# Block 2's second product in a fused retention and feed-forward kernel: from eight block products to seven

## The chip, the cores and the metric

The kernel runs on one core of a Trainium2 chip. The metric is the device time of one execution in microseconds (us). Before the change it is 290.14 us, the median of 3 runs (290.06 to 290.16). The engines are called by the profile's names: PE (TensorE, matrix products), PEld (its weight loads), DVE (VectorE), ACT (ScalarE), POOL (GpSimd) and SP (SyncE, which here only issues DMA transfers, in its program's order).

## The reference

For 8 batches, 8 heads, 576 positions and head width 64, the attention part is retention: scores without softmax, damped by a power of the distance. Its result, as 4608 rows of 512, goes through a feed-forward layer of width 2048 with the activation h / (1 + exp(-beta h)).

```python
scores = (1 / sqrt(64)) * q @ k.T                    # per batch and head
ret = scores * where(i >= j, gamma[head] ** (i - j), 0)
x = (ret @ v)                                        # heads side by side: 4608 x 512
h = x @ w_in                                         # 4608 x 2048
g = h / (1 + exp(-beta * h))
out = g @ w_out                                      # 4608 x 512
```

Inputs and output are float32; the kernel multiplies in bfloat16.

## The kernel before

**Blocks.** The rows are worked on in nine blocks of 512. Blocks 0 to 7 are the first 512 positions of each batch, block 8 is the last 64 positions of all eight. For each block m, `up` (L773) makes the first product: 16 pieces (`fo`) of 128 columns of width 2048, each 4 matmuls of 512 columns into a PSUM bank of tag `mm`, of which there are three; ACT reads the bank, applies the activation (L790) and writes the piece of `gT` in bfloat16. In block 1 the first ten pieces are done in two halves of 256 columns (L1026).

**The second product in two ways.** For blocks before `SB` (L50, here 3: blocks 0 to 2), `down` (L901) makes `out = g @ w_out` with 64 matmuls of 512 columns (L908), ACT or DVE copies each finished bank to `ot` (L915), and SP stores it. From block `SB` on, the product is cut into 2 x 2 quarters and made from seven products of sums of quarters instead of eight (Strassen's method, in a form that needs few sums): `seven_mm` (L809), 7 x 16 matmuls of 256 columns (L820), on sums of the quarters of `gT` (`seven_a`, L798, DVE) and sums of the quarters of `w_out` (`seven_b`, L239), and `seven_out` (L825) combines the results on ACT and DVE. In these blocks the odd pieces of `gT` get an extra scaling on DVE by a ratio of betas, by way of a scratch buffer `hs` (L785 to L788).

**The weight sums** are made once, for four groups g of `w_out` rows. For each group, `scale_w_out` scales four float32 tiles in place on ACT (L237), `seven_b` makes five sums on DVE (L254) and two negated copies on ACT (L250), and `last_seven` (L256) gives the float32 tile back. The sums of group 0 have a place of their own; those of groups 1 to 3 take the buffers that the float32 tiles of groups 0 to 2 leave (tag `wt`), and `hs` takes that of group 3. The sums of `gT` take the place of `w_out_sb`, the plain bfloat16 weights (tag `wo`), which `cast_w_out` (L222) has made in block 0.

**Attention.** The attention of batch b is computed while block b-1 is in work, in between the large matmuls. `load_q` (L77) and `load_kv` (L89) bring its inputs; POOL scales and casts them (`pre_q` L322, `pre` L342); `x_q` and `x_k` (L403, L406) have the DMA engines transpose them; `scores` (L615) makes the scores of one or both pairs of chunks and the states of four chunks; DVE masks the scores (L298 stands for all steps that are recorded through the helper `F` there) and sums the states (`fold`, L590), whose bfloat16 copies ACT or DVE makes; `both4` (L708) makes outputs and cross terms, and writes the block's `xT`. `first_states` (L607) makes the first four states of a batch by themselves; `crosses4` otherwise makes those of the next batch along with the cross terms (L687). In the first two batches other functions do the same with transposes on PE (`t_q`, `t_k`, L413, L420; `a_sc`, L434; `state_out`, L534; `second`, L1038).

**The order.** Each engine works through its instructions in the program's order. That order is written by hand: `fill` is a list of positions, each a few large matmuls, and `streams` are lists of (position, step); `merged` (L928) puts each step ahead of the first `fill` entry whose index is not below its position. `d0` is the first position of block 0's second product, `u1 = d0 + 16` the start of block 1, `base[n]` the start of block n, and `base[2] = u1 + 42`, called T in the prediction. A `down` block has 16 + 16 positions, a seven-product block 16 + 14. Batch n+1's preparation is placed by `pair_prep` (L1067) relative to `at` (L1137 to L1141), its scores at `base[n] + lead[n]` from block `SB` on (L1109), and the transpose of its second pair by `asked` (L1112). `release` (L897) stores four held-back pieces of the output of blocks 0 and 1.

Of the kernel before, what the change touches and what calls it, by code (L numbers as in the profile page):

```python
# [19 lines left out]
def kernel(  # L20
# [11 lines left out]
    B, H, S, D = q.shape  # L32
# [14 lines left out]


    blocks = list(range(B + 1))
    SB = 3  # L50
    KH = FO // 2
    NH = d_model // 2
    seven = (3, 4, 1, 5, 2, 7, 6)
# [19 lines left out]
    XB = 2  # L73
# [65 lines left out]
    for j, (steps, mul) in enumerate((([[2, 2], [1, 2]], CB), ([[2 * P, 2], [1, 2]], 2))):  # L139
        nc.gpsimd.iota(pos[:, j, :CB].rearrange("p (a r) -> p a r", r=2), pattern=steps, base=0, channel_multiplier=mul,  # L140
                       allow_small_or_imprecise_dtypes=True)
        for x in range(2):
            nc.gpsimd.iota(pos[x * TL:(x + 1) * TL, j, CB:CB + 1], pattern=[[0, 1]], base=MB, channel_multiplier=1,
                           allow_small_or_imprecise_dtypes=True)
            for m, base in ((0, TL), (1, x * P)):
                nc.gpsimd.iota(pos[x * TL:(x + 1) * TL, j, CB + 1 + 2 * m:CB + 3 + 2 * m], pattern=[[2 * P, 2]],
                               base=x * TL + base, channel_multiplier=1, allow_small_or_imprecise_dtypes=True)
# [40 lines left out]
    WG = 4  # L188
# [108 lines left out]
    def F(f, *a):  # L297
        return lambda: f(*a)  # L298
# [291 lines left out]
    def fold(b, e, bank, ns=range(4), casts=None, by=None):  # L590

        for n in ns:
# [5 lines left out]
            else:  # L598
                nc.vector.tensor_tensor(ends[b][:], of, new, ALU.add)
                return  # L600
            cast = F(by or (nc.vector.tensor_copy if b > SB else nc.scalar.copy), sbq[e + n], to)
            if casts is not None:
# [165 lines left out]


    gts = {}  # L770
    halved = (12, 13, 14, 15)

    def up(m, fo, c0=0, cn=CB):  # L773
        if m not in gts:
            gts[m] = sb.tile([P, FO, CB, P], BF16, name="gT", tag="gT", bufs=1)
        w = slice(c0 * PC, (c0 + cn) * PC)
        ph = psum.tile([P, CB, P], F32, name="ph", tag="mm", bufs=3)
        ph = ph.rearrange("f i s -> f (i s)")[:, :cn * P].rearrange("f (i s) -> f i s", i=CB)
        ns = 2 if m == SB and fo in halved or m == 1 and 10 <= fo < 13 else 1
        for ko in range(KO):  # L780
            for n in range(ns):
                cs = slice(n * CB // ns, (n + 1) * CB // ns)
                nc.tensor.matmul(ph[:, cs], w_in_sb[:, ko, fo * P:(fo + 1) * P], xts[m][:, ko, cs, w],  # L783
                                 start=(ko == 0 and n == 0), stop=(ko == KO - 1), skip_group_check=ns > 1)
        if m >= SB and fo % 2:  # L785
            h = scratch[0][:, fo // 2 % 4].rearrange("f (i s) -> f i s", i=CB)
            nc.scalar.activation(h, ph, ACT.Silu, scale=beta_sb[:, fo:fo + 1])  # L787
            nc.vector.tensor_scalar(gts[m][:, fo], h, ratio[:, fo // 2:fo // 2 + 1], None, ALU.mult)  # L788
            return
        nc.scalar.activation(gts[m][:, fo, :, w], ph, ACT.Silu, scale=beta_sb[:, fo:fo + 1])  # L790
# [224 lines left out]
    d0 = len(fill)  # L1015
# [9 lines left out]
    u1 = len(fill)  # L1025
# [3 lines left out]
    base = {1: u1 + 10}  # L1029
# [37 lines left out]
    def pair_prep(i, at):  # L1067
        b, c = seq[i]
        if b is None:
            if c:  # L1070
                return [(at - 27, F(load_tail, c)), (at - 20, F(load_tail, c + 1)), (at - 17.5, F(pre, i)),
                        (at - 12, F(pre, i + 1)), (at - 12, F(x_tail, i)), (at - 9.5, F(x_tail, i + 1))]
            return [(at - 31, F(load_tail, c)), (at - 21.5, F(pre, i)), (at - 21, F(load_tail, c + 1)),
                    (at - 13, F(pre, i + 1)), (at - 12, F(x_tail, i)), (at - 9.5, F(x_tail, i + 1))]
        n, st = full.index(i), []
        if b == XB:
            if c == 0:
                return [(d0 + 13, F(pre, i + x, (0,))) for x in range(2)] + \
                       [(d0 + 14, F(pre, i + x, (1,))) for x in range(2)]
            return [(u1 + 8 + x / 2, F(pre, i + x)) for x in range(2)]  # L1080
        if c == 0:
            st += [(at - 30, F(x_k, XB, 1))] if b == XB + 1 else []
            st += [(at - 30, F(load_q, b))] + [(at - 20 + x, F(pre_q, b, x)) for x in range(4)]
            st += [(at - 14 + 1.5 * x, F(x_q, b, x)) for x in range(2)]
            return st + [(at - 28, F(load_kv, n)), (at - 26, F(load_kv, n + 1)), (at - 16, F(pre, i)),
                         (at - 15, F(pre, i + 1)), (at - 11.5, F(x_k, b, c // 2))]
        turned_at = asked[b + 1] - 30.1
        st += [(turned_at - 0.4 + 0.1 * x, F(pre, i + x, (0,))) for x in range(2)]
        st += [(turned_at, F(x_k, b, c // 2))] + [(turned_at + 0.1 + 0.1 * x, F(pre, i + x, (1,))) for x in range(2)]
        return st + [(at - 29.3, F(load_kv, n)), (at - 29.2, F(load_kv, n + 1))]  # L1090

    def span(a, n, by=1.0):
        return [a + by * x for x in range(n)]

    sums_b = (3, 4, 1, 7, 6)
    t = base[2]
    by_scalar = [span(t - 15.5, 4, 0.8), span(t - 12, 4, 0.8), [t - 9.7, t - 9.4, t - 9.1, t - 3.6], span(t + 16.5, 4, 0.7)]
    by_vector = [span(t - 11, 5, 1.4), span(t - 3, 5, 1.5), span(t + 4.5, 5, 1.8), span(t + 19.6, 5, 1.4)]
    negated = [(t - 3.8, t - 3.4), (t + 0.5, t + 2.5), (t + 16.1, t + 16.2), (t + 21, t + 23)]
    for g in range(WG):  # L1100
        streams.append([(x, F(scale_w_out, g, i)) for i, x in enumerate(by_scalar[g])])
    streams.append(sorted([(x, F(seven_b, g, j)) for g in range(WG) for xs, js in ((by_vector[g], sums_b), (negated[g], (2, 5)))
                           for x, j in zip(xs, js)] +
                          [(max(by_vector[g][-1], negated[g][-1]) + 0.1, F(last_seven, g)) for g in range(WG)], key=lambda x: x[0]))

    def queued(at, steps):
        return [(x, lambda: steps.pop(0)()) for x in at]

    lead = dict(zip(range(SB, B - 1), (7, 4, 2, 1)))  # L1109
    lead[B - 1] = 5  # L1110
    behind = dict(zip(range(SB, B - 1), (0, 0, 1, 0)))
    asked = {n + 1: base[n] + (lead[n] - 13 if n in lead else 3) for n in range(XB, B - 1)}  # L1112
    asked[B] = base[B - 2] + lead[B - 2] + 19

# [2 lines left out]
    for n in range(SB, B + 1):  # L1117
        t, m = base[n], blocks[n]
        first, second = slice(0, KH // 2), slice(KH // 2, KH)
        if n == SB:  # L1120
            halves = [(t + 14.4, 1, first), (t + 15.1, 5, first), (t + 16.3, 1, second), (t + 16.4, 5, second)] + \
                     [(t + 17.5 + 0.5 * x, j, ks) for x, (j, ks) in enumerate((j, ks) for j in (2, 7) for ks in (first, second))]
        else:
            early = [t + 11.4, t + 12.6, t + 15.3, t + 15.4] if n == SB + 1 else [t + 9.8, t + 10.8, t + 11.8, t + 14.4] if n < B else span(t + 9, 4)
            halves = [(x, j, first) for x, j in zip(early, (1, 5, 2, 7))] + [(t + 16.4 + 0.1 * x, j, second) for x, j in enumerate((1, 5, 2, 7))]
        streams.append([(x, F(seven_a, m, j, ks)) for x, j, ks in halves] +
                       [(t + 22.1, F(seven_a, m, 6))])

    todo = list(range(2 * CB, len(seq), 2))
    for n in range(1, B):  # L1130

        take = [i for i in todo if seq[i][0] == n + 1 or n == B - 1]
        todo = todo[len(take):]
        b, t = n + 1, base[n]
        t0 = t + lead.get(n, 0)
        if n == 1:
            at = [t + 17, base[b] - 8.3]  # L1137
        elif n < SB:
            at = [t + 3, t + 18]
        else:  # L1140
            at = [t0 - 13, t0 + 2] if n < B - 1 else [t0 - 9.5, t0 - 2.5]  # L1141
        for i, x in zip(take, at, strict=True):
            streams.append(pair_prep(i, x))
        if n == 1:
            streams.append([(d0 + 6.1, F(mask, late, [1, CB], [CB, PC // 2])),
                            (d0 + 6.2, F(mask, tri, [1, TL]))])
            streams.append([(at[0], F(group1, b, (0,))), (at[1], F(group1, b, (1,))), (at[1] + 4.1, F(both4, b))])
        elif n < SB:
            streams.append([(t + 16, F(first_states, b))] * (b == XB + 1) +
                           [(t + 19, F(group1, b, (0, 1))), (t + 25.9, F(both4, b))])  # L1150
        elif n == B - 1:
            outs = []
            streams.append([(t0, F(tail_scores, take[0])), (t + 13, F(both_tails, take[0], outs))] +
                           queued([t + 16.3, t + 17.6, t + 20.5, t + 22.5], outs))
        else:
            rest, outs = [], []
            t0 -= behind[n]
            if b == SB + 2 and SB == XB + 1:
                streams.append([(t - 4, F(first_states, b))])
            streams.append([(t0, F(scores, b, (0, 1), rest))] + queued([t0, t0 + 0.9, t0 + 1.7, t0 + 2.6, t0 + 3.4, t0 + 4.2, t0 + 4.3, t0 + 5.1, t0 + 6] if n == SB else  # L1160
                           [t0, t0 + 0.9, t0 + 0.9, t0 + 1.8, t0 + 2.6] + span(t0 + 3.4, 4, 0.9), rest))
            by = t + 17.4 if n == SB else t + 14.5 if n == SB + 1 else t + 12.8
            streams.append([(by, F(both4, b, outs))] + queued([t + 16.3 + 2 * (n == SB)] * 4 + [t + 17.3, t + 18.3, t + 20.3, t + 20.4][:0 if n in (SB, B - 2) else 4], outs))
    assert not todo
    merged(fill, *streams)

# [29 lines left out]
```

## Time and profile before

| | us |
|---|---|
| median of 3 runs | 290.14 (290.06 to 290.16) |
| the profiled execution, whole | 289.33 |
| its span in the profile | 287.6 |
| block 0's second product starts | 32.0 |
| block 1 starts | 49.8 |
| block 1's second product starts | 66.7 |
| block 2 starts | 83.5 |
| block 3 starts | 114.5 |
| block 4 starts | 143.8 |

The page of the profile gives the busy time of each engine, the groups of instructions and the chain of waits, which is followed back from the last instruction to what released each step. A group is "line, engine, operation, output <- inputs, shape, count | busy us, mean ns". The mean of a matmul is its latency (379 ns at 512 columns); matmuls follow each other more closely than that, so their spacing is read from the chain. In a timeline a line is "start, length, engine, line, operation, count, and in brackets the idle time before it with what ended it". `SPq` is the queue on which SP issues transfers; there the length is the time of the issue, not of the transfer. Windows are in us from the start of the span. The granted clock of PE is 1.00 all through.

### The profile page before, as it was taken

The page shows a single profiled execution, that of the slowest core. Times are in us where ns is not written, and L with a number is a line of the kernel's source. Part 1 is how long each engine was busy: PE and PEld are TensorE (multiplying, and loading weights), DVE is VectorE, ACT ScalarE, POOL GpSimd, SP SyncE. Part 2 cuts the span into 40 slices and gives each one's busy share as a digit, 9 for nine tenths or more (in the row PEclk, how much of TensorE's full clock was granted, in tenths as well). Part 3 has the DMA queues.
Part 4 walks back from the last instruction along what each step waited for, and adds up shares of the span by engine and source line. Part 5 has one row for each costly group of instructions (what it writes and reads, how often), then busy time and mean ns, then how long its engine had stood idle before and what let it go on. Part 6 is the DMA issues. An engine that isn't in the chain of part 4 may idle for free.

```text
span 287.6 us, 8701 instructions
## 1 busy us (share of the span) xinstructions
PE 278.9 (97%) x3618; PEld 177.2 (62%) x3648; DVE 185.3 (64%) x345; ACT 169.7 (59%) x298; POOL 132.3 (46%) x259
## 2 busy tenths in 40 slices
PE   7899999999999999999999999999999999999995
PEld 3564456884454455568854885578557845884584
DVE  5973546704797296289759856885698455742673
ACT  4567635686968882775358615681566166827730
POOL 7466019933991684195595476533089200000000
PEclk9999999999999999999999999999999999999999
DMA  7999999977899999999998998950779330012004
GB/s 224 306 364 386 382 310 294 178 160 208 168 184 264 244 186 210 291 212 191 194 260 212 181 269 249 197 116 0 230 168 156 87 136 3 2 46 100 2 7 139
DMA packets 120567, 54.05 MB, mean 188 GB/s; under 512 B 93888, under 2 KB 113360, under 8 KB 120528
## 3 DMA queue, kind: packets, MB, share of 16 engines
q1 hardware_dynamic: 120496, 53.49, 78.0%
q8 instruction: 28, 0.46, 0.7%
q14 instruction: 11, 0.09, 0.1%
q10 hardware_dynamic: 32, 0.01, 0.0%
HBM read 36.71 MB, written 9.44 MB: 160 GB/s over the span
## 4 chain that ended last, share of the span: by engine, by line
PE 94%; DMA 3%; issue 1%; SPq 1%; ACT 0%; POOL 0%; DVE 0%; ACTq 0%
PE ph L783 39%; PE po L908 14%; PE U L820 11%; PE Z L820 7%; PE W L820 7%; PE O L561 4%; PE ph L875 4%; DMA kvn<-in_k_dram 3%; PE sc L561 2%; PE st L561 2%; PE st L521 1%; PE ph L890 1%; PE T L425 1%; PE O L488 1%; SPq L86 0%
## 5 line engine op out<-in xcount | busy, mean ns | idle before, releaser
L783 PE MATMUL ph<-xT,w_in_sb 128*128 128x512 bf16 (+1 forms) x570 | 114.2, 354 | 0.9
L783 PEld LDWEIGHTS <-w_in_sb 128*128 128x128 bf16 x588 | 56.4, 98 | 52.1 <-DVE xT L694 0.2
L790 ACT ACTIVATE gT<-ph,beta_sb 128x512 bf16<-128x512 f32 (+1 forms) x92 | 58.2, 640 | 39.2 <-PE ph L783 38.1
L820 PEld LDWEIGHTS <-sa 128*128 128x128 bf16 x480 | 46.9, 98 | 5.5
L788 DVE TENSOR_SCALAR gT<-hs,ratio 128x512 bf16<-128x512 f32 x48 | 27.1, 565 | 31.2 <-ACT hs L787 30.7
L335 POOL TENSOR_TENSOR qs<-qn,gq 128x256 bf16<-128x256 f32 x48 | 29.9, 655 | 33.5 <-DMA qn<-in_q_dram 29.2
L787 ACT ACTIVATE hs<-ph,beta_sb 128x512 f32<-128x512 f32 x48 | 33.0, 687 | 18.9 <-PE ph L783 18.3
L908 PE MATMUL po<-w_out_sb,gT 128*128 128x512 bf16 x183 | 42.0, 379 | 1.0 <-issue 0.8
L804 DVE TENSOR_TENSOR sa<-gT 128x1024 bf16<-128x1024 bf16 (+1 forms) x54 | 41.6, 812 | 0.8 <-PE Z L820 0.6
L317 POOL TENSOR_TENSOR vn<-kvn,gv 128x256 bf16<-128x256 f32 x48 | 33.2, 715 | 3.0 <-issue 2.0
L372 POOL CAST kn<-kvn 128x128 bf16<-128x128 f32 (+1 forms) x72 | 25.1, 386 | 14.8 <-DMA kvn<-in_k_dram 14.7
L908 PEld LDWEIGHTS <-gT 128*128 128x128 bf16 x192 | 18.0, 97 | 20.8
L820 PE MATMUL Z<-b,sa 128*128 128x256 bf16 x192 | 22.9, 273 | 0.0
L820 PE MATMUL U<-b,sa 128*128 128x256 bf16 x192 | 22.9, 273 | 0.0
L298 DVE TENSOR_TENSOR R<-sc,late 128x512 bf16<-128x512 f32 x24 | 15.4, 679 | 11.3 <-issue 10.1
L820 PEld LDWEIGHTS <-gT 128*128 128x128 bf16 x192 | 18.7, 98 | 3.2
L254 DVE TENSOR_TENSOR b<-wt 128x512 bf16<-128x512 f32 x20 | 15.6, 840 | 1.9 <-ACT wt L237 1.8
L694 ACT CAST xT<-O 128x512 bf16<-128x512 f32 x19 | 9.8, 599 | 5.9 <-PE O L561 5.9
L384 POOL CAST kn<-kvn 128x512 bf16<-128x512 f32 x7 | 4.4, 647 | 16.0 <-DMA kvn<-in_k_dram 16.0
L820 PE MATMUL W<-b,gT 128*128 128x256 bf16 x96 | 11.5, 273 | 0.0
L820 PE MATMUL W<-b,sa 128*128 128x256 bf16 x96 | 11.5, 273 | 0.0
L820 PE MATMUL U<-b,gT 128*128 128x256 bf16 x96 | 11.5, 273 | 0.0
(122 smaller groups left out, 313.4 us busy)
## 6 DMA issues: line engine op xcount, KB each, us to landing
qn<-in_q_dram SPq DMA_DIRECT2D x16, 512.0 KB, 5.8
out_dram<-ot SPq DMA_DIRECT2D x32, 256.0 KB, 3.1
wt<-in_moe_w_out_dram SPq DMA_DIRECT2D x8, 512.0 KB, 9.2
kvn<-in_k_dram SPq DMA_DIRECT2D x12, 256.0 KB, 5.4
kvn<-in_v_dram SPq DMA_DIRECT2D x12, 256.0 KB, 6.2
kvn<-in_k_dram SPq DMA_DIRECT2D x24, 128.0 KB, 5.0
kvn<-in_v_dram SPq DMA_DIRECT2D x24, 128.0 KB, 4.1
wt<-in_moe_w_in_dram SPq DMA_DIRECT2D x5, 512.0 KB, 8.8
```

Source lines behind the costliest of these rows:

```text
L254: nc.vector.tensor_tensor(to, x, y, op)
L317: nc.gpsimd.tensor_tensor(vn[:, hs], v[:, hs], g[:, hs], ALU.mult)
L335: nc.gpsimd.tensor_tensor(batch[b]["qs"][:, cs, to], q_tiles[b][:, hs, cs].rearrange("p h i d -> p i h d"), gq[:, cs, hs].unsqueeze(3).to_ ...
L372: nc.gpsimd.tensor_copy(kn[:, c % 2, to], t[:, 0, hs])
L561: ins = nc.tensor.matmul(out, lhsT, rhs, start=start, stop=stop, skip_group_check=True)
L783: nc.tensor.matmul(ph[:, cs], w_in_sb[:, ko, fo * P:(fo + 1) * P], xts[m][:, ko, cs, w], start=(ko == 0 and n == 0), stop=(ko == KO - 1), ...
L787: nc.scalar.activation(h, ph, ACT.Silu, scale=beta_sb[:, fo:fo + 1])
L788: nc.vector.tensor_scalar(gts[m][:, fo], h, ratio[:, fo // 2:fo // 2 + 1], None, ALU.mult)
L790: nc.scalar.activation(gts[m][:, fo, :, w], ph, ACT.Silu, scale=beta_sb[:, fo:fo + 1])
L804: nc.vector.tensor_tensor(sums_a[0][:, held_in[j], ks], quarter(m, *x, ks), quarter(m, *y, ks), op)
L820: nc.tensor.matmul(chains[c, n][:, 0 if alone else p], a, sevens[k // 2][:, j - 1, k % 2, :], start=j in (3, 4, 1) and k == 0 and (alone o ...
L908: nc.tensor.matmul(po[:, :nn], gT[:, fo, ms, :], w_out_sb[:, fo, n0:n0 + nn], start=(fo == 0), stop=(fo == FO - 1))
```

## The change

`SB` becomes 2, so block 2 also makes its second product by seven products. The weight sums of all groups are now made between `d0 + 3` and T - 5, in the second product of block 0 and in block 1; before, they went on until block 2's second product. The scores of batch 3 move from T + 19 to T + 9 and its `both4` from T + 25.9 to T + 17.4; its `first_states` from T + 16 to T + 3. Its loads and transposes move forward: `load_q(3)` and two `load_kv` now stand at u1 + 15, just ahead of the transpose of batch 2's second pair, which stood ahead of them. Batch 4's scores go from position 7 of block 3 to position 6, and as block 2 is two positions shorter, all that is placed by later blocks moves with them. The splitting of pieces 12 to 15 of block `SB` into halves of 256 columns is dropped.

```diff
@@ -47,7 +47,7 @@
 
 
     blocks = list(range(B + 1))
-    SB = 3
+    SB = 2
     KH = FO // 2
     NH = d_model // 2
     seven = (3, 4, 1, 5, 2, 7, 6)
@@ -768,7 +768,6 @@
 
 
     gts = {}
-    halved = (12, 13, 14, 15)
 
     def up(m, fo, c0=0, cn=CB):
         if m not in gts:
@@ -776,7 +775,7 @@
         w = slice(c0 * PC, (c0 + cn) * PC)
         ph = psum.tile([P, CB, P], F32, name="ph", tag="mm", bufs=3)
         ph = ph.rearrange("f i s -> f (i s)")[:, :cn * P].rearrange("f (i s) -> f i s", i=CB)
-        ns = 2 if m == SB and fo in halved or m == 1 and 10 <= fo < 13 else 1
+        ns = 2 if m == 1 and 10 <= fo < 13 else 1
         for ko in range(KO):
             for n in range(ns):
                 cs = slice(n * CB // ns, (n + 1) * CB // ns)
@@ -1079,11 +1078,14 @@
                        [(d0 + 14, F(pre, i + x, (1,))) for x in range(2)]
             return [(u1 + 8 + x / 2, F(pre, i + x)) for x in range(2)]
         if c == 0:
-            st += [(at - 30, F(x_k, XB, 1))] if b == XB + 1 else []
-            st += [(at - 30, F(load_q, b))] + [(at - 20 + x, F(pre_q, b, x)) for x in range(4)]
+            if b == XB + 1:
+                st += [(base[b - 1] + x, F(load_q, b)) for x in (-27,)] + [(base[b - 1] - 26.9 + x / 10, F(load_kv, n + x)) for x in range(2)]
+                st += [(base[b - 1] - 26.7, F(x_k, XB, 1))]
+            else:
+                st += [(at - 30, F(load_q, b))] + [(at - 28, F(load_kv, n)), (at - 26, F(load_kv, n + 1))]
+            st += [(at - 20 + x, F(pre_q, b, x)) for x in range(4)]
             st += [(at - 14 + 1.5 * x, F(x_q, b, x)) for x in range(2)]
-            return st + [(at - 28, F(load_kv, n)), (at - 26, F(load_kv, n + 1)), (at - 16, F(pre, i)),
-                         (at - 15, F(pre, i + 1)), (at - 11.5, F(x_k, b, c // 2))]
+            return st + [(at - 16, F(pre, i)), (at - 15, F(pre, i + 1)), (at - 11.5, F(x_k, b, c // 2))]
         turned_at = asked[b + 1] - 30.1
         st += [(turned_at - 0.4 + 0.1 * x, F(pre, i + x, (0,))) for x in range(2)]
         st += [(turned_at, F(x_k, b, c // 2))] + [(turned_at + 0.1 + 0.1 * x, F(pre, i + x, (1,))) for x in range(2)]
@@ -1094,21 +1096,23 @@
 
     sums_b = (3, 4, 1, 7, 6)
     t = base[2]
-    by_scalar = [span(t - 15.5, 4, 0.8), span(t - 12, 4, 0.8), [t - 9.7, t - 9.4, t - 9.1, t - 3.6], span(t + 16.5, 4, 0.7)]
-    by_vector = [span(t - 11, 5, 1.4), span(t - 3, 5, 1.5), span(t + 4.5, 5, 1.8), span(t + 19.6, 5, 1.4)]
-    negated = [(t - 3.8, t - 3.4), (t + 0.5, t + 2.5), (t + 16.1, t + 16.2), (t + 21, t + 23)]
+    by_scalar = [[d0 + 3, d0 + 3.1, d0 + 3.2, d0 + 6], span(d0 + 6.1, 4, 0.1), [d0 + 12.2, d0 + 12.3, u1 + 9.5, u1 + 9.6],
+                 span(t - 16, 4, 0.1)]
+    by_vector = [[d0 + 8, d0 + 8.1, d0 + 8.2, u1 + 10.1, u1 + 10.2], span(u1 + 10.3, 5, 0.1), span(u1 + 21.2, 5, 0.1),
+                 span(t - 11, 5, 1.5)]
+    negated = [(d0 + 12.1, d0 + 12.15), (u1 + 20.1, u1 + 21.1), (t - 16.2, t - 16.1), (t - 13, t - 12)]
     for g in range(WG):
         streams.append([(x, F(scale_w_out, g, i)) for i, x in enumerate(by_scalar[g])])
     streams.append(sorted([(x, F(seven_b, g, j)) for g in range(WG) for xs, js in ((by_vector[g], sums_b), (negated[g], (2, 5)))
                            for x, j in zip(xs, js)] +
-                          [(max(by_vector[g][-1], negated[g][-1]) + 0.1, F(last_seven, g)) for g in range(WG)], key=lambda x: x[0]))
+                          [(max(by_vector[g][-1], negated[g][-1]) + 0.05, F(last_seven, g)) for g in range(WG)], key=lambda x: x[0]))
 
     def queued(at, steps):
         return [(x, lambda: steps.pop(0)()) for x in at]
 
-    lead = dict(zip(range(SB, B - 1), (7, 4, 2, 1)))
+    lead = dict(zip(range(SB, B - 1), (9, 6, 4, 2, 1)))
     lead[B - 1] = 5
-    behind = dict(zip(range(SB, B - 1), (0, 0, 1, 0)))
+    behind = dict(zip(range(SB, B - 1), (0, 0, 0, 1, 0)))
     asked = {n + 1: base[n] + (lead[n] - 13 if n in lead else 3) for n in range(XB, B - 1)}
     asked[B] = base[B - 2] + lead[B - 2] + 19
 
@@ -1121,7 +1125,7 @@
             halves = [(t + 14.4, 1, first), (t + 15.1, 5, first), (t + 16.3, 1, second), (t + 16.4, 5, second)] + \
                      [(t + 17.5 + 0.5 * x, j, ks) for x, (j, ks) in enumerate((j, ks) for j in (2, 7) for ks in (first, second))]
         else:
-            early = [t + 11.4, t + 12.6, t + 15.3, t + 15.4] if n == SB + 1 else [t + 9.8, t + 10.8, t + 11.8, t + 14.4] if n < B else span(t + 9, 4)
+            early = [t + 12.6, t + 13.4, t + 15.3, t + 15.4] if n == 3 else [t + 11.4, t + 12.6, t + 15.3, t + 15.4] if n == 4 else [t + 9.8, t + 10.8, t + 11.8, t + 14.4] if n < B else span(t + 9, 4)
             halves = [(x, j, first) for x, j in zip(early, (1, 5, 2, 7))] + [(t + 16.4 + 0.1 * x, j, second) for x, j in enumerate((1, 5, 2, 7))]
         streams.append([(x, F(seven_a, m, j, ks)) for x, j, ks in halves] +
                        [(t + 22.1, F(seven_a, m, 6))])
@@ -1155,12 +1159,14 @@
         else:
             rest, outs = [], []
             t0 -= behind[n]
-            if b == SB + 2 and SB == XB + 1:
+            if n == XB:
+                streams.append([(t + 3, F(first_states, b))])
+            if b == SB + 2:
                 streams.append([(t - 4, F(first_states, b))])
             streams.append([(t0, F(scores, b, (0, 1), rest))] + queued([t0, t0 + 0.9, t0 + 1.7, t0 + 2.6, t0 + 3.4, t0 + 4.2, t0 + 4.3, t0 + 5.1, t0 + 6] if n == SB else
                            [t0, t0 + 0.9, t0 + 0.9, t0 + 1.8, t0 + 2.6] + span(t0 + 3.4, 4, 0.9), rest))
-            by = t + 17.4 if n == SB else t + 14.5 if n == SB + 1 else t + 12.8
-            streams.append([(by, F(both4, b, outs))] + queued([t + 16.3 + 2 * (n == SB)] * 4 + [t + 17.3, t + 18.3, t + 20.3, t + 20.4][:0 if n in (SB, B - 2) else 4], outs))
+            by = t + {2: 17.4, 3: 16, 4: 14.5}.get(n, 12.8)
+            streams.append([(by, F(both4, b, outs))] + queued([t + {2: 18.3, 3: 17.3}.get(n, 16.3)] * 4 + [t + 17.3, t + 18.3, t + 20.3, t + 20.4][:0 if n in (SB, B - 2) else 4], outs))
     assert not todo
     merged(fill, *streams)
 
```

## The prediction, made before the result was known

> **What bounds the kernel now.** I read the page first, then the chain of waits, then the stretches block by block, then the engines' own timelines around the blocks that the edit touches. Times are in us; T is the start of block 2 (`base[2]`, 83.5 in the trace); "T-8.3" counts list positions, 0.87 us each where one position is four 512-wide matmuls, 0.44 in the half-width part of block 1.
>
> ```profile
> span 287.6 us, 8701 instructions
> PE 278.9 (97%) x3618; PEld 177.2 (62%) x3648; DVE 185.3 (64%) x345; ACT 169.7 (59%) x298; POOL 132.3 (46%) x259
> ...
> PE 94%; DMA 3%; issue 1%; SPq 1%; ACT 0%; POOL 0%; DVE 0%; ACTq 0%
> ```
>
> TensorE is busy for 97% and is 94% of the chain; what remains is mostly the first 10 us. So the time moves by what TensorE executes, plus any wait that the edit puts in front of it. The chain in order of time has the two forms of the second product:
>
> ```profile
> 80.24 3.40 PE po L908 x15
> ...
> 129.65 1.75 PE U L820 x16
> ```
>
> The stretches by block (columns: window, length, busy time of PE, PEld, DVE, ACT, POOL) show blocks 2, 3 and 4:
>
> ```profile
> 83.30:114.60 31.30, 30.88 (x407) 15.36 (x410) 21.19 (x38) 22.29 (x39) 17.92 (x34) 1.00 1.02 217
> 114.60:143.80 29.20, 29.05 (x439) 21.03 (x441) 20.91 (x37) 16.92 (x28) 16.57 (x28) 1.00 1.03 224
> 143.80:172.60 28.80, 28.64 (x421) 19.50 (x424) 20.54 (x38) 15.90 (x27) 19.01 (x37) 1.00 1.14 230
> ```
>
> **The gain on TensorE.** Removed: 64 matmuls of 512 columns in block 2. Forty of them stand in one piece of the chain in block 0, 8.64 long from 32.20: 0.216 each, so 13.83. Added: 7 products of 16 matmuls at 1.75, so 12.25. Difference -1.58. The clean way to count the rest is by whole blocks. With `SB = 2` block 2 is built as block 3 was (seven products, the attention of the next batch without the states "ahead", `first_states` for the batch after it), plus one `first_states(3)` of 32 small matmuls (0.38 in the chain). Block 3 is built as block 4 was. Before: 31.1 (83.48 to 114.58) + 29.2 = 60.3. After: 29.2 + 0.4 + 28.8 = 58.4. Gain **-1.85**; the extra 0.27 is the dearer interleaving of crosses with states in old block 2 (1.9 against 1.6 in block 4). Splitting `up` of block 3 at 12 to 15 goes: 32 x 0.109 = 3.49 becomes 16 x 0.216 = 3.46, nothing (-0.1 to +0.1). The additions in block 2 on DVE (8 scalings at 0.49 to 0.78, nine sums of gT, five combinations at 0.69) are what block 3 carried with DVE busy for 20.9 of 29.2 and no TensorE wait; scores come two positions later against the same `both4`, which leaves about 1 us of the margin between the last sum (130.2) and the crosses (131.9): 0, up to 0.3.
>
> **Where the weight sums go.** The 20 L254 sums, 16 L237 scalings and 8 L250 negations are the same in number. In blocks 2 and 3 they cost nothing before and save nothing now. What counts is what they push aside in blocks 0 and 1.
>
> (a) *Three L254 ahead of the turned queries (d0+8).* DVE is free at 41.10 and its next work, the two qT copies, starts at 43.04. An L254 took 0.70 with GpSimd idle (7 in 4.90 from 86.75) and 0.95 beside it, so three take 2.1 to 2.85, and the copies start 0.2 to 0.9 late; they and the kT copy end 1.47 after that. TensorE started these scores at 44.69, 0.18 after the kT copy, and only their second half reads that copy. Stall 0 to 0.9; I take **+0.5**. GpSimd runs casts then, so the dearer row is nearer.
>
> Here the Trainium skill speaks against the change (SBUF — State Buffer, section "Who interferes with whom"): a vector instruction with two SBUF inputs and a GpSimd instruction that reads SBUF do not share; one blocks fully until the other is done. This trace is milder: beside each other from 83.6 to 87.3 an L254 took 0.95 and a GpSimd L317 0.92, where taking turns would be 0.70 + 0.59 = 1.29. By the rule the sum would be higher; it is a rival below.
>
> (b) *ACT in block 0.* Scalings follow each other at 0.62 (ten in 6.23). Three fall before the last w_out cast at 36.77, five after it, to about 40.7; the first po copy was at 40.87. Two negations and two scalings go behind the kT copy, 44.30 + 2.4 = 46.7, and the state copies were at 47.14. Idle ACT covers all of it (it waited 3.38 before that po copy and 2.84 before the state copies): 0, and up to 0.3 where it falls short.
>
> (c) *Two scalings at u1+9.5, in the half-width part.* This is the row that decides:
>
> ```profile
> 56.86 5.28 ACT L790 ACTIVATE gT<-ph,beta_sb 128x256 bf16<-128x256 f32 x12 [1.56 <-PE ph L783]
> ...
> 71.65 6.23 ACT L237 ACTIVATE wt<-wt,rbeta_sb 128x512 f32<-128x512 f32 x10
> ```
>
> ACT takes 0.44 per half-width piece, TensorE 0.437 (48 matmuls in 5.24): ACT has no slack. Two scalings are 1.25. `ph` has three banks: piece 13 needs the bank of piece 10. Piece 10's activation started at 57.74 and would start at 58.99 and end at 59.46; TensorE would have begun piece 13 at 58.40. Stall **+1.1** (0.2 if one more bank's worth were free, 1.25 at most). Behind it wait all later activations; nothing later on TensorE is idle to give it back. The negations at u1+20.1 and 21.1 stand one full piece apart, where ACT needs 0.69 of 0.865; a lag of up to 0.75 stays inside the banks, the first uses 0.6, the second as much again less 0.18: 0 to 0.2, I take 0. Seven DVE sums there fit its 10.1 us of idle time before 68.19. The five for group 2 write into the buffer that group 1 leaves once it is negated, near 66.2, and so end near 70.4; the masks of batch 2's first pair and the first po copy slip by less than 1, and that copy's bank is wanted 2 later: 0. From T-16 to T ACT has 8 such insertions where it had 14, and DVE five sums where it had seven: 0.
>
> (d) *`first_states(3)` at T+3 instead of T+16.* At 97.38 the old one kept ACT from its other work until 100.18, 2.80 after its first matmul, since the four casts wait for the DVE sums. Now activations of block 2 queue behind them. Three pieces of 0.865 and the 0.45 of the states cover 3.04; the activation whose bank is wanted ends at 2.80 + 0.69 + 0.05 = 3.54. Stall **+0.5** (0 to 0.8).
>
> (e) *Batch 3's loads ahead of batch 2's second transpose on SP.*
>
> ```profile
> 61.16 1.31 SPq L103 DMA_DIRECT2D kvn<-in_v_dram  x2
> 64.92 1.24 SPq L401 DMA_TRANSPOSE kT<-kn  x1
> 66.26 1.10 SPq L86 DMA_DIRECT2D qn<-in_q_dram  x2
> ...
> 73.91 1.31 SPq L103 DMA_DIRECT2D kvn<-in_v_dram  x2
> ```
>
> The transpose issued at 64.92; now `load_q(3)` and two `load_kv` stand before it. Issuing those took 66.26 to 75.22, 9.0. SP is free at 62.47, so the transpose issues at about 71.4 (72.5 if the queue is fuller) and lands 3.1 to 4.6 later, say 75.7. Its scores ran at 74.45; with (a) and (c) TensorE comes at 76.05. So **+0.1**, bounds 0 and +1.5. Without (a) and (c) it would itself cost 1.2. Behind it on SP: kv 14 and 15 (5.5), x_q(3) (3.3), two transposes: the last lands near 88, its scores at T+9 run near 94. Margin 6: 0. GpSimd's scaling of batch 3's queries (4.9) starts when the load lands, near 68, and ends by 75, ahead of SP's need at 78. The four stores at T-4.5 now follow that transpose, `load_q(4)` and a `load_kv`; their buffer is wanted near 104: 0. Batch 4's transfers, its states in block 3 and the stores at T+21 move by 2 to 3 positions with block 3, as 8 us lay between the last transpose of batch 4 (109.9) and its scores (120.7): 0.
>
> **Sum.** -1.85 + 0.5 + 1.1 + 0.5 + 0.1 = +0.35, on the profiled execution's 289.33 (span 287.6 and 1.7 around it): 289.7. That execution lies 0.8 below the median of 290.14; I carry the difference to the median: **290.5**. A measurement of this kernel tells about 0.2%, 0.6 us, from no change, so the forecast is "no change", on its upper side.
>
> **Rivals.**
> 1. *The stalls are covered, the gain stays* (chance 0.28): if (c) costs 0.2, (a) 0.3 and (d) nothing, -1.35, 288.8. For it: ACT has 1.56 idle just before 56.86. Against: the scalings stand behind that idle time in ACT's order.
> 2. *The transpose lands late* (0.18): the place is scores(2, 1) at T-8.3; it decides once the landing passes 76.05. At 77.6 (issue 73.0, landing 4.6) it adds 1.5: 292.0, slower. For it: one pair of issues alone held SP for 4.85 at 69.02. Against: DMA engines were almost idle from 64.5 to 66.2.
> 3. *DVE and GpSimd take turns* (0.07): the three L254 at (a) alternate with two casts of 0.585, 3 x 0.70 + 1.17 = 3.3, kT copy at 45.9, stall up to 1.1: 291.1. This is the skill's rule above.
> 4. *The change doesn't do what it says in time* (0.05): the last sums or the scratch buffer (which takes the last weight tile's place) aren't ready at T+1. DVE ends them near 83.2 and the shifted T+1 is near 86; at 5 us late, +2.5 beyond the forecast: 293.0.
>
> My forecast has 0.42, its own range 289.9 to 291.2. About 0.27 of it lies within 0.2% and 0.15 above. Rival 1 is faster but for 0.02. So faster 0.26, same 0.29, slower 0.45. The range from 288.6 to 292.1 leaves out the lower end of rival 1 and most of rival 4, under 0.2.
>
> **What would show it.** Right: block 2 near 29.6 without its stalls; a TensorE wait of about 1 us near 58 to 60 in block 1 that ends on ACT; one of 0.5 on a DVE copy near 45; one of 0.5 four to six pieces into block 2. Wrong: the scores of batch 2's second pair waiting for DMA; no wait in block 1 at all; TensorE waiting in block 3, which I cost at nothing.

## The result, and the profile after

The changed kernel takes 291.94 us (median of 6 runs, 291.32 to 292.76) against 290.12 (6 runs, 289.89 to 290.53): ratio 1.0062, 95% interval 1.0044 to 1.0081. It is slower by 1.8 us. The ratio, here and below, is that of the fast runs and not of the two medians. The time lies in the predicted range, but the forecast was 290.5: a step that it had put at 0 to 0.3 cost 0.8 to 1.5, and one that it had put at 0.5 cost next to nothing in most profiles.

The profiled execution after took 292.76, the longest of the six, and its span is 291.0. Starts of the stages, read from the PE timelines of both kernels, give these lengths in us:

| stage | before | after |
|---|---|---|
| start to block 0's second product | 32.0 | 32.7 |
| block 0's second product | 17.8 | 17.8 |
| block 1's first product | 16.8 | 17.8 |
| block 1's second product | 16.8 | 17.2 |
| block 2 | 31.0 | 32.0 |
| block 3 | 29.3 | 29.0 |
| block 4 | 28.8 | 29.1 |
| the rest | 115.0 | 115.4 |

The first row is the scatter of the first loads (the one that the chain goes through took 7.5 before and 8.4 after): in all the other profiles of this study the stage takes 32.3 to 33.0, so the profiled execution of before had an early start, and 3.4 us between the two spans overstates the change. Three rows differ most: block 1's first product (+1.0), its second (+0.4), and block 2, which was to become 1 us shorter (31.1 to 30.1, with a stall of 0.5) and became 1 us longer. The 0.4 lies in the crosses at 80 to 82, where the profile shows 0.2 of idle time that it puts down to no engine; the profiles of casts_dve, stores_late and no_scaled_v below, in which PE has the same work there, have 16.9 to 17.0 for this stage, so most of it is scatter.

The page shows the shift in two lines: the engines' shares of the span, and their shares of the chain that ended last.

```profile
PE 278.6 (96%) x3652; PEld 180.6 (62%) x3680; DVE 201.4 (69%) x364; ACT 169.7 (58%) x300; POOL 136.1 (47%) x259
...
PE 84%; DVE 7%; DMA 3%; ACT 2%; issue 1%; SPq 1%; POOL 0%; DVEq 0%; ACTq 0%
```

PE's busy time is almost that of before (278.6 against 278.9) and tells little. The chain tells more: PE no longer makes nearly all of it, and DVE, which had 0%, has 7%. The chain in order of time (start, length, step) tells where. First in block 1:

```profile
56.93 0.56 PE ph L782 x4
57.51 0.91 ACT gT L789 x2
58.42 1.22 ACT wt L237 x2
59.64 0.37 ACT gT L789
60.05 6.05 PE ph L782 x53
```

The two scalings stand between two activations, and PE goes on only when the third one has freed its bank. Then in block 2:

```profile
104.91 0.52 issue
105.42 2.14 DVE sa L803 x3
107.57 0.27 issue
107.83 3.13 DVE sa L803 x3
110.97 0.61 DVE ot L833
111.62 1.91 PE U L819 x16
```

The fifth product adds to a bank (chain U) that DVE must first have read (L833), and that reading stands in DVE's order behind seven sums of the quarters of gT. The waits of PE, by what ended them (total, times, longest), put numbers to both:

```profile
PE U L819 <- DVE ot L833: 1.7, 2, 1.5
...
PE ph L782 <- ACT gT L789: 0.8, 1, 0.8
...
PE ph L782 <- ACT hs L786: 0.3, 1, 0.3
```

The last of the three is the place of `first_states(3)`. The timelines of DVE and POOL show what the seven sums ran beside (one fence for each engine):

```profile
104.62 6.35 DVE L803 TENSOR_TENSOR sa<-gT 128x1024 bf16<-128x1024 bf16 x7
```

```profile
106.32 4.10 POOL L317 TENSOR_TENSOR vn<-kvn,gv 128x256 bf16<-128x256 f32 x4
```

Both are slow: a sum took 0.68 at its fastest and 1.10 here (median of the line's nine), an L317 0.59 alone and 1.03 here. Before, in block 3, GpSimd's work of the same kind fell later against the sums: its L317 began when the seven sums, which took 4.87, were done.

```profile
131.52 4.87 DVE L804 TENSOR_TENSOR sa<-gT 128x1024 bf16<-128x1024 bf16 x7
136.32 0.68 DVE L834 TENSOR_TENSOR ot<-ot,U 128x512 f32<-128x512 f32 x1
```

```profile
136.75 3.75 POOL L317 TENSOR_TENSOR vn<-kvn,gv 128x256 bf16<-128x256 f32 x4
```

### The profile page after: what moved, and what is told of

Same layout as the page of the kernel before. It is cut to its first block, busy times and chain, and to the rows that moved or that the text cites. A ratio compares the mean times of both kernels' runs of the same rounds, so it can differ in the third digit from the quotient of the medians.

```text
span 291.0 us, 8797 instructions
## 1 busy us (share of the span) xinstructions
PE 278.6 (96%) x3652; PEld 180.6 (62%) x3680; DVE 201.4 (69%) x364; ACT 169.7 (58%) x300; POOL 136.1 (47%) x259
## 4 chain that ended last, share of the span: by engine, by line
PE 84%; DVE 7%; DMA 3%; ACT 2%; issue 1%; SPq 1%; POOL 0%; DVEq 0%; ACTq 0%
PE ph L782 36%; PE U L819 12%; PE po L907 9%; PE Z L819 7%; PE W L819 6%; DVE sa L803 4%; PE ph L874 4%; PE O L561 3%; DMA kvn<-in_k_dram 3%; PE sc L561 2%; PE st L561 2%; DVE gT L787 1%; DVE R L298 1%; PE st L521 1%; ACT hs L786 1%
## 5 line engine op out<-in xcount | busy, mean ns | idle before, releaser
L789 ACT ACTIVATE gT<-ph,beta_sb 128x512 bf16<-128x512 f32 (+1 forms) x84 | 52.6, 636 | 44.0 <-PE ph L782 42.9
L819 PEld LDWEIGHTS <-sa 128*128 128x128 bf16 x560 | 54.7, 98 | 8.3 <-issue 2.0
L787 DVE TENSOR_SCALAR gT<-hs,ratio 128x512 bf16<-128x512 f32 x56 | 30.3, 542 | 35.7 <-ACT hs L786 35.1
L803 DVE TENSOR_TENSOR sa<-gT 128x1024 bf16<-128x1024 bf16 (+1 forms) x63 | 51.6, 860 | 1.3 <-PE Z L819 1.1
L786 ACT ACTIVATE hs<-ph,beta_sb 128x512 f32<-128x512 f32 x56 | 38.5, 687 | 19.9 <-PE ph L782 19.4
L335 POOL TENSOR_TENSOR qs<-qn,gq 128x256 bf16<-128x256 f32 x48 | 34.2, 743 | 22.0 <-DMA qn<-in_q_dram 11.3
L317 POOL TENSOR_TENSOR vn<-kvn,gv 128x256 bf16<-128x256 f32 x48 | 32.9, 708 | 5.9 <-issue 3.9
L907 PE MATMUL po<-w_out_sb,gT 128*128 128x512 bf16 x122 | 28.2, 379 | 0.6 <-issue 0.5
L819 PE MATMUL U<-b,sa 128*128 128x256 bf16 x224 | 26.7, 272 | 1.7 <-DVE ot L833 1.7
L819 PE MATMUL Z<-b,sa 128*128 128x256 bf16 x224 | 26.8, 273 | 0.0
L819 PEld LDWEIGHTS <-gT 128*128 128x128 bf16 x224 | 21.7, 98 | 3.9
L907 PEld LDWEIGHTS <-gT 128*128 128x128 bf16 x128 | 12.0, 98 | 13.7
L254 DVE TENSOR_TENSOR b<-wt 128x512 bf16<-128x512 f32 x20 | 16.7, 890 | 2.7 <-ACT b L250 2.6
L384 POOL CAST kn<-kvn 128x512 bf16<-128x512 f32 x7 | 5.3, 781 | 17.3 <-DMA kvn<-in_k_dram 17.3
```

The lines of the kernel that those rows point to most:

```text
L317: nc.gpsimd.tensor_tensor(vn[:, hs], v[:, hs], g[:, hs], ALU.mult)
L335: nc.gpsimd.tensor_tensor(batch[b]["qs"][:, cs, to], q_tiles[b][:, hs, cs].rearrange("p h i d -> p i h d"), gq[:, cs, hs].unsqueeze(3).to_ ...
L803: nc.vector.tensor_tensor(sums_a[0][:, held_in[j], ks], quarter(m, *x, ks), quarter(m, *y, ks), op)
L819: nc.tensor.matmul(chains[c, n][:, 0 if alone else p], a, sevens[k // 2][:, j - 1, k % 2, :], start=j in (3, 4, 1) and k == 0 and (alone o ...
L907: nc.tensor.matmul(po[:, :nn], gT[:, fo, ms, :], w_out_sb[:, fo, n0:n0 + nn], start=(fo == 0), stop=(fo == FO - 1))
```

## The experiments

After the first comparison two theories stood for block 2: **theory 1**, the scores' place alone (T+9 against position 7 in old block 3) makes DVE late; **theory 2**, GpSimd's work beside the sums slows them. Block 1's stall and the small ones were tested with them. All times below are against the kernel before, run on the same chip.

**sums_only.** The new `by_scalar`, `by_vector` and `negated` lists, with the 0.05 of `last_seven`, put into the kernel before, and nothing else.

> The kernel before with one part of the change alone: the weight sums, scalings and negations at their new places in blocks 0 and 1; block 2 still makes its second product by the 64 large matmuls, and the attention stays where it was. Theory (stalls in block 1): the two scalings at u1+9.5 hold ACT, TensorE waits 0.8 to 1.1 us near 58 to 60, and the three sums at d0+8 cost 0 to 0.5; nothing in block 2 to give back, so 290.12 + 0.8 to 1.6 = 290.9 to 291.7. Rival (all that was lost is lost in block 2): the sums are covered, within 0.3 us of before.

291.41 against 290.03, ratio 1.0062 (1.0038 to 1.0086). Block 1's first product took 17.8, as in the full change. The other stages from block 0's second product to block 4 took what they had taken before, to within 0.2. The wait is the same one:

```profile
PE ph L783 <- ACT gT L790: 0.8, 1, 0.8
```

So moving the weight sums costs time by itself: 1.0 by this stage, 1.4 by the medians, 1.8 by the ratio (1.1 to 2.5), which one run of six at 293.57 may lift. What lies above 1.0 is not placed. The stage of the three sums at d0+8 took 17.8, no more than before.

**scale_early.**

```diff
-    ... [d0 + 12.2, d0 + 12.3, u1 + 9.5, u1 + 9.6],
+    ... [d0 + 12.2, d0 + 12.3, u1 + 7.6, u1 + 7.7],
```

> The changed kernel with one edit: the two scalings of group 2 stand at u1+7.6, ahead of the eighth half-width piece, where ACT sat idle for 1.56 us, and not at u1+9.5. Theory (they stall TensorE through the three banks): the wait of 0.84 us near 59 goes, and 291.94 becomes 290.9 to 291.2. Rival (the time then reappears at the scores of batch 2's second pair, whose transpose lands at 75.7 and which would now come at 75.2): 291.4 to 291.9.

290.54 against 290.03, 1.0018 (1.0003 to 1.0033): 1.3 below the changed kernel by the ratios, more than expected. Block 1's first product is back at 16.8 and the wait is gone. The rival showed in a corner: PE now waited 0.3 for the transpose of batch 2's second pair. The wait for L833 in block 2, which the edit does not touch, was 1.0 in this profile in place of 1.5, so not all of the 1.3 has to come from block 1.

**lead7.**

```diff
-    lead = dict(zip(range(SB, B - 1), (9, 6, 4, 2, 1)))
+    lead = dict(zip(range(SB, B - 1), (7, 6, 4, 2, 1)))
```

> The changed kernel with batch 3's scores at T+7 in place of T+9 (and what is placed relative to them two positions earlier too); SP's order is the same. Theory 1 (VectorE is late in block 2 because the scores come two positions later than in old block 3): the wait of TensorE for VectorE ahead of the fifth product, 1.5 us, goes, 290.4 to 290.9. Theory 2 (VectorE is late because its sums of gT run beside GpSimd's work, 1.10 us each against 0.68): the sums stay slow, and at most 0.5 us is gained, 291.4 to 291.9.

290.93 against 290.03, 1.0041 (1.0020 to 1.0062). The wait for L833 is gone in the trace and block 2 takes 29.9; yet the sums stayed slow (median 0.88, seven in 5.70). They only began earlier: 2.0 behind the start of the block's first product of the seven, against 3.1. The median lies just above theory 1's range, and the interval of the ratio overlaps that of the changed kernel, so the time does not decide; the trace says that both hold: an earlier start covers the slow sums. The profile also shows where a part of the gain went: block 1's second product took 17.7, 0.5 more, with a wait of PE of 0.3 for the transpose of batch 2's second pair.

**stores_late.**

```diff
-                (base[2] - 4.5, F(release, 4))],
+                (base[2] + 9, F(release, 4))],
```

> The changed kernel with the four held-back stores of block 0 at T+9, after batch 4's loads on SP, in place of T-4.5, ahead of two of them. These issues held SP for 4.5 us, and GpSimd's work on batch 4's second pair waited for loads behind them and then ran beside VectorE's sums of gT. Theory 2 (that overlap slows the sums): the sums fall from 1.10 to 0.7 to 0.8 us, the wait ahead of the fifth product shrinks by 1.0 to 1.5, 290.5 to 291.0. Theory 1 (lateness of the scores alone): no change, 291.7 to 292.1.

291.39 against 290.03, 1.0052 (1.0032 to 1.0071), between the two. The sums stayed at a median of 1.10, so what theory 2 expected of them did not come; but GpSimd's scaling began earlier (102.97), the seven sums began 0.7 earlier against their products and took 5.96, and the wait shrank from 1.5 to 0.3. The edit moved the overlap and didn't remove it, and so it could not separate the theories.

**no_scaled_v.** This one leaves out the four L317 that ran beside the sums, and so the scaling of batch 4's second pair, and leaves the scores at T+9. GpSimd's casts still run beside the first sums.

```diff
     def pre(i, js=(0, 1)):
...
         if 0 not in js:
+            if b == XB + 2 and c >= 2:
+                kv_tiles.pop(i)
+                nc.gpsimd.memset(live[i]["vn"][:], 1.0)
+                return
```

> The changed kernel with part of GpSimd's work left out: the values of batch 4's second pair of chunks are not scaled but set to one, by a write that reads nothing from SBUF (so batch 4's outputs are not the reference's); the scores stay at T+9. Theory 2 (VectorE's sums of gT in block 2 are slow because GpSimd's scaling, 4.1 us from 106.3, runs beside them): the seven sums take 4.9 to 5.6 us in place of 6.35, VectorE's combination of the third chain comes 0.8 to 1.4 earlier, and TensorE's wait of 1.5 ahead of the fifth product falls to 0.1 to 0.7; 290.6 to 291.3. Theory 1 (the scores' place alone makes VectorE late): the seven sums take 6.0 or more, the wait stays above 1.0, 291.6 to 292.2.

290.50 against 290.24, 1.0018 (1.0001 to 1.0036). The timelines of DVE and POOL, with the line numbers of this kernel:

```profile
103.74 4.68 DVE L807 TENSOR_TENSOR sa<-gT 128x1024 bf16<-128x1024 bf16 x7
108.34 0.67 DVE L837 TENSOR_TENSOR ot<-ot,U 128x512 f32<-128x512 f32 x1
```

```profile
103.45 2.02 POOL L376 CAST kn<-kvn 128x256 bf16<-128x256 f32 x3 [1.23 <-DMA kvn<-in_k_dram]
105.41 0.98 POOL L348 MEMSET vn<- 128x512 bf16 x2
```

The seven sums take 4.68 in place of 6.35, somewhat less than expected, and PE has no wait for DVE left in block 2. The scores' place was not touched. In the three profiles with scores, stores and L317 in place (the changed kernel, scale_early, casts_dve) the sums took 6.0 to 6.35 and the wait was 0.8 to 1.5. Theory 2 is shown for the delay; theory 1 stands as the other half: with the scores two positions earlier the margin is wide enough for slow sums.

**casts_dve.**

```diff
-        fold(b, 0, bank, casts=casts, by=nc.scalar.copy)
+        fold(b, 0, bank, casts=casts, by=nc.vector.tensor_copy if b == XB + 1 else nc.scalar.copy)
```

(in `first_states`)

> The changed kernel with one edit: the four casts of first_states(3) at T+3 are made on VectorE, which idles there, in place of ACT. Theory (ACT's activations queue behind the casts, and TensorE waits 0.33 us for a bank at 91.3): that wait goes, 291.94 becomes 291.3 to 291.7. Rival (VectorE's extra 1.4 us delays the scaling of odd pieces or its later backlog): 291.9 to 292.5.

291.71 against 290.27, 1.0042 (1.0027 to 1.0056). The time alone does not decide, as its interval overlaps that of the changed kernel; the chain and block 2's first product (15.4 in place of 16.0) do. PE goes straight on behind the states, where it stood for DVE and ACT from 88.75 to 91.67, 0.3 longer than its three pieces:

```profile
88.50 0.38 PE st L561 x32
88.88 5.29 PE ph L782 x24
```

The same profile shows something that no other does: block 0's second product took 18.8 in place of 17.8. The chain now runs through a load of queries that landed at 40.75:

```profile
29.57 11.18 DMA qn<-in_q_dram
```

So the three sums at d0+8 began at 41.99, and they ran slower (2.73) than in the changed kernel (from 41.26, 2.30), beside casts of GpSimd whose load had come late too:

```profile
41.99 2.73 DVE L254 TENSOR_TENSOR b<-wt 128x512 bf16<-128x512 f32 x3
```

```profile
42.54 1.63 POOL L384 CAST kn<-kvn 128x512 bf16<-128x512 f32 x2 [12.99 <-DMA kvn<-in_k_dram]
```

PE waited 0.3 for the second cast and 0.3 for the kT copy behind the sums:

```profile
46.03 0.53 PE L561 MATMUL sc<-qT,kT 64*64 64x128 bf16 x24 [0.30 <-DVE kT L426]
```

This is the stall of the prediction's step (a). The edit does not touch block 0.

**two_fixed** (scale_early and lead7 together).

> The changed kernel with the two scalings at u1+7.6 and batch 3's scores at T+7. Theory (the two stalls, 0.95 in block 1 and 1.0 to 1.5 in block 2, are separate): the gains add, less about 0.3 that comes back as a wait for the transpose of batch 2's second pair; 289.3 to 290.0. Rival (both edits buy the same time, as the scores that come a microsecond earlier wait for loads): 290.4 to 290.9, no better than the better of the two alone.

289.76 against 290.27, 0.9982 (0.9970 to 0.9993). The gains add, and what comes back is the transpose, issued behind batch 3's loads; now it is on the chain:

```profile
71.10 4.60 DMA kT<-kn
75.75 0.45 PE sc L561 x32
```

PE waited 0.8 for it, more than the 0.3 expected.

**four_fixed** (and casts_dve, and the transpose behind `load_q(3)` alone).

```diff
-                st += [(base[b - 1] - 26.7, F(x_k, XB, 1))]
+                st += [(base[b - 1] - 26.95, F(x_k, XB, 1))]
```

> As two_fixed, and the casts of first_states(3) on VectorE, and the transpose of batch 2's second pair on SP behind load_q(3) alone, ahead of the two load_kv. Theory (0.3 each): no wait is left that before did not have, and the gain of seven products, 1.85 less 0 to 0.5, stands: 288.3 to 289.2. Rival (the transpose holds SP, and batch 3's own loads come late for scores at T+7): a wait for DMA near 92 and 289.5 to 290.5.

289.09 against 290.27, 0.9955 (0.9938 to 0.9972): faster than before by 1.3. Blocks 1 and 2 are without a wait of PE in the list; the chain runs through block 2 on PE alone:

```profile
106.89 1.75 PE W L819 x16
108.64 1.75 PE U L819 x16
```

**five_fixed** (and stores_late).

> As four_fixed, and the four held-back stores at T+9. Theory: with the scores at T+7 VectorE is in time already, so no more than 0.2 us is gained, 288.2 to 289.2, though the margin between VectorE's combination of the third chain and the fifth product grows by about 1 us in the trace. Rival (in most executions the wait in block 2 is still there with the scores at T+7): 0.4 to 1.0 us below four_fixed.

289.73 against 290.27, 0.9990 (0.9970 to 1.0010): no gain over four_fixed, rather a loss, so neither the theory nor its rival came true. In its profile a new wait of 0.7 stands in block 2, for ACT's copy of chain W (L832), which began at 106.03, 1.5 after ACT's work before it. The profile names a product of chain Z for ACT's wait, but the copy reads chain W, whose product had ended at 104.3. The copy writes the output buffer that the four stores read, and these were now issued at 99.30 to 101.8. That it waited for them is argued, not tried.

## Why the prediction was right in range and wrong in sum

- **What bounds the kernel**: held. Every change of time that could be placed was a wait of PE or PE's own work.
- **The gain of 1.85**: held within 0.4. With the waits removed (four_fixed) blocks 2 and 3 take 29.8 and 29.1, 58.9 in place of 60.3 before, and the whole is 1.3 lower. Its block 4 took 29.2, 0.4 more than before, and there was a wait of 0.2 on a sum of gT.
- **(a) three sums ahead of the turned queries, +0.5**: came to 0 in the profiled execution, to 0.15 or less in eight of the other nine profiles that have these sums there, and to 1.0 in that of casts_dve. In the profiled execution they took 2.30, near the cheaper end, and ended at 43.56; the copies were then 0.65 behind the start of PE's transposes, as they had been before (0.64). What decides is when the loads of the queries land against PE: the sums began 8.4 to 8.8 behind the start of block 0's second product in those nine, and 9.7 behind it in casts_dve. In the one profile that the step was read from, DVE was free 9.1 behind that start, between the two. The row was right, and its execution was not the typical one.
- **(b) ACT in block 0, 0**: held; the state copies of batch 1 waited for PE, not for ACT.
- **(c) two scalings in the half-width part, +1.1**: held, 1.0. Shown from both sides, by sums_only and scale_early.
- **(d) `first_states(3)`, +0.5**: right place; 0.3 as a wait of PE, 0.5 by the length of block 2's first product with and without the casts on ACT.
- **(e) the transpose behind the loads, +0.1**: held. It was issued at 71.43 and landed 4.3 later, at 75.7 as forecast, and the scores came at 76.2. With (c) gone PE waited 0.3 and 0.8, where the prediction had said 1.2 without (a) and (c). In lead7, with (c), it waited 0.3.
- **The step that failed**: "what block 3 carried with DVE busy for 20.9 of 29.2 and no TensorE wait; scores come two positions later [...] 0, up to 0.3". It cost a wait of 1.5 in block 2 of the profiled execution, 1.0 and 0.8 in those of scale_early and casts_dve, and 0.2 in block 4. The count of DVE's instructions was right. The two positions were weighed against the crosses alone (130.2 to 131.9). Ahead of the fifth product there was less: before, L834 ended at 137.0 and that product began at 137.9. In new block 2 the sums began 1.1 later against their products (0.7 in casts_dve), which took most or all of these 0.9. What was carried over unseen was when GpSimd works: in old block 3 its four long L317 began at 136.75, when the seven sums were done; in new block 2 they began at 106.32, inside them. The sums grew by 1.5 (4.87 to 6.35), and the two positions given up for the scores had used the margin that would have covered a part of it. So the additions were not hidden: DVE came late, by both together.
- **The rivals**: none came true as told. The time is that of rival 2, but the transpose was in time. Rival 3's mechanism, DVE and GpSimd in each other's way, was the right one at the wrong place: at the casts of block 0 it cost PE nothing in the profiled execution. In casts_dve's the kT copy did end at 46.0, about where this rival has it, but more by late loads than by taking turns, as the sums took 2.73 and not 3.3. The Trainium skill (SBUF — State Buffer, section "Who interferes with whom") says that of a vector instruction with two SBUF inputs and a GpSimd one that reads SBUF one blocks until the other is done. For the sums of gT this trace comes nearer to it than before: taking turns would give 0.68 + 0.59 = 1.27 for a pair, and a sum took 1.10 beside an L317 of 1.03. And GpSimd's write that reads nothing left the sums at 4.68. I had weighed the rule only where the diff adds sums, not where it moves old ones.
- **The sum with what was measured**: a gain of 1.4, and against it 1.0 for (c), 0.8 to 1.5 in block 2 and 0.3 to 0.5 for (d) make +0.7 to +1.6. The measured +1.8 has an interval of 1.3 to 2.3; what is left, if anything, is not placed.

## What to carry to other kernels

A block that is to be built "as the next one is" does not inherit that block's waits: check for each pair of engines that slow each other when the partner works, which the landing of its loads decides here. A stage where ACT needs as long per piece as PE has no room for a single extra instruction, however idle ACT is on average; 1.25 us put in there cost 1.0, and two positions earlier nothing. And read a margin of half a microsecond from more than one execution: the start of this kernel alone scatters by more, and a stall that was at most 0.15 in nine profiles took 1.0 in the tenth.

## What the runs showed of the hardware that was not expected

Which of two engines loses when both work on SBUF inputs depends on the instructions, and for one pair on the execution. In block 0 the three L254 sums took 2.30 beside casts of GpSimd (0.70 each alone), and two L384 casts took 2.11 (1.17 before, alone); in casts_dve the same sums took 2.73 and the casts 1.63. Beside the sums of gT in bfloat16, three casts (L376 in no_scaled_v) took 2.02 where three took 0.87 earlier in the block, and the sums lost nothing, at 0.68 each. Beside an L317 both lost: a sum took 1.10 against 0.68, and the L317 1.03 against 0.59.
